# One FFN input chunk in two parts around an attention product, in a fused linear-attention and FFN kernel

## The chip, the core and the metric

The kernel runs on one core of a Trainium2 chip. The metric is the device time of one execution in microseconds. Five engines work side by side, each with an instruction queue of its own: TensorE (PE; its weight loads are shown as PEld), VectorE (DVE), ScalarE (ACT), GpSimd (POOL) and SyncE (SP, which here only issues transfers). All times below are in microseconds.

## The reference

A linear attention over 8 batches of 8 heads, 576 positions and 64 features, and behind it an FFN with an ELU between its two products.

```python
q_s = exp(q - max(q, -1));  q_s = q_s / (sum(q_s, -1) + 1e-9)
k_s = exp(k - max(k, 2));   k_s = k_s / (sum(k_s, 2) + 1e-9)
kv = einsum('bhsd,bhse->bhde', k_s, v)
attn = einsum('bhsd,bhde->bhse', q_s, kv)
x = attn.transpose(0, 2, 1, 3).reshape(4608, 512)
h = x @ w_in                                  # 512 -> 2048
g = where(h > 0, h, exp(min(h, 0)) - 1)
out = g @ w_out                               # 2048 -> 512
```

## The kernel before

**Steps.** The program goes batch by batch, and each batch (j from 0) in 16 steps, one for each chunk of 128 of the 2048 hidden features; 16 more steps at the end handle the positions that each batch leaves over. Chunks are numbered through: n = 16 j + c, so that chunk 16 is the first one of the second batch. Each chunk has four pieces of work:

- *h(n)*, the FFN input product (hidden_mm, L912): four matmuls, kc = 0 to 3, each contracting 128 of the 512 model features and all adding up in one PSUM bank (banks 0 to 2 by turns). Matmul kc reads quarter kc of the batch's attention output, tile XT.
- *E(n)*, the exponential on ACT (L895, for some chunks L892 and L893) and, for the L895 chunks, a subtraction of 1 on POOL (L896), into tile ES.
- *elu(n)* on VectorE (L925), which joins the two into tile GT.
- *p(n)*, the output product (project, L933): four matmuls, t = 0 to 3, which add onto banks 3 to 6, where a batch's output grows over its 16 chunks.

TensorE's order is h(n) and then p(n - 3), step by step: h15, p12, h16, p13, h17, p14 and so on. After p15 the first batch's output is complete, and its four banks are evicted, banks 3 and 5 by ACT (L942), banks 4 and 6 by VectorE (L944), and stored by SP. p16 is the first product that writes these banks again, behind h19.

**The attention of the next batch** runs in the gaps of these steps. Its last part is four products, att:f (attend, L805), one matmul each, which all write bank 7, and four copies, xc:f (xcopy, L814, on ACT), which bring bank 7 to quarter f of XT. Since they share the bank, att:f waits for the xc before it. They come in the order 0, 1, 3, 2.

**The order** on every engine is written out by hand. A table (FIRST for the steps of the first batch, SECOND for the second's) gives for each step three lists of words: the first is done behind h(n) and its E(n), the second behind p(n - 3), the third behind elu(n). An engine's queue is in program order. One semaphore wait stands ahead of each instruction that needs another engine's result.

In the last two steps of FIRST there are also, for the third batch: join2 (kpeak_join, a chain of small VectorE operations that ends in tile KU, L413), kout2 (kpeak_out, L417: a transfer of KU to memory, issued from ACT's queue), and load:V:2:MR (transfers on SP's queue). In the first steps of SECOND VectorE takes the maxima of queries (qmax, L672) and POOL subtracts them (qsub, L679).

Of the kernel before, what the change touches and what calls it, by code (L numbers as in the profile page):

```python
# [14 lines left out]
NCH = DFF // 128  # L15
# [10 lines left out]
LAG = 3  # L26
HELD = ((8, 6), (8, 9), (8, 12))
HB = (0, 1, 2)
EARLY = 4
FINE = 1  # L30
OB = (3, 4, 5, 6)
# [32 lines left out]
    12: ("pturn:B w2:15:16", "pwide:B:act load:Q:2:ABR", "w2:13:15"),  # L64
    13: ("kv:A vconv:B:dve", "kfac:A:dve", "kexp:B peak2:B att:0 xc:0"),
    14: ("kv:B kfac:B:dve peak2:R qmulr:gp", "att:1 peak2:A", "join2 turn:R xc:1"),
    15: ("att:3", "xc:3", "att:2 load:V:2:MR xc:2 kout2"),
}
SECOND = {
    0: ("qmax:C qsub:D", "", "qmax:A"),  # L70
# [50 lines left out]
class Gen:  # L121
# [754 lines left out]
    def hbank(self, n):  # L876

        if n < EARLY:
            return HB[n] if n < len(HB) else AB
        return HB[(n - EARLY) % len(HB)]  # L880

    def hidden(self, j, c):

        a, g = self.E["act"], self.E["gp"]
        n = j * NCH + c
        bank = self.hbank(n)
        ps, ES = self.bank[bank], self.ES[n % NE]
        self.hidden_mm(j, c, range(2, 4) if n < EARLY else range(4))
        for x, keys in self.pieces("ES", n, NE):
            mark = ["FINE"] if n < FINE else []  # L890
            if n in AT["clip"]:
                self.op("act", lambda: a.activation(ES[:, x], ps[:, x], AF.Relu, scale=-1.0), [f"bank{bank}"], keys + mark)  # L892
                self.op("act", lambda: a.activation(ES[:, x], ES[:, x], AF.Exp, scale=-1.0), keys, keys)  # L893
                continue
            self.op("act", lambda: a.activation(ES[:, x], ps[:, x], AF.Exp), [f"bank{bank}"], keys + mark)  # L895
            self.op("gp", lambda: g.tensor_scalar(ES[:, x], ES[:, x], -1.0, 1.0, ALU.add, ALU.mult),  # L896
                    keys, keys)
# [6 lines left out]
    def hidden_mm(self, j, c, kcs):  # L904
        pe = self.E["pe"]
        bank = self.hbank(j * NCH + c)
        x = self.XT[j % 2] if j < B else self.XTR
        xkeys = [self.xkeys(j, (f,), "LH") for f in range(4)] if j < B else [[f"XTR{b}" for b in range(B)]] * 4
        ps = self.bank[bank][:, :]
        for kc in kcs:  # L910
            def mm():
                return pe.matmul(ps, self.W1S[:, kc, c * 128:(c + 1) * 128], x[:, kc, 0:SM],  # L912
                                 start=(kc == 0), stop=(kc == 3))
            self.hidden_done = self.op("pe", mm, xkeys[kc] + [f"W1_{c}"],
                                       [f"bank{bank}"])

# [67 lines left out]
    def finish(self, first):  # L984
# [7 lines left out]
        for t in range(3):  # L992
# [3 lines left out]
            self.store_rest(t, "sp")  # L996
        for i, bank in enumerate((HB[0], AB)):
            for c in last:
# [147 lines left out]
    def program(self):  # L1146
        self.alloc()
        self.init()
        self.first_batch()

        steps = [(j, s) for j in range(B + 1) for s in range(NCH)]
        behind = 0
        for i, (j, s) in enumerate(steps):
            mid, end, after = TABLES.get(j, LATER).get(s, NONE) if j < B else NONE
            self.hidden(j, s)
            self.do(j, mid)
            if i >= LAG and (j, s) not in HELD:
                pj, ps = steps[behind]
                behind += 1
                self.project(pj, ps)  # L1160
                self.do(j, end)
                if ps == NCH - 1:
                    self.store(pj)
            else:
                self.do(j, end)
            self.elu(j, s)
            self.do(j, after)
        self.finish(steps[behind][1])
        for name in self.sems:
            if name.startswith("d_OSB"):  # L1170
                self.E["sp"].wait_ge(self.sems[name], self.count[name])
# [36 lines left out]
```

## Time and profile before

| what | value |
|---|---|
| runs shown | 308.54, 308.96 (median), 309.47 |
| the profiled execution | 309.2, of which the span of the profile is 307.4 |
| granted TensorE clock | 1.0 of full speed |
| TensorE busy | 298.6 |
| VectorE, ACT, POOL busy | 234.8, 193.1, 171.8 |
| where chunk 16 lies in the span | h16 from 53.92, E16 from 55.56, elu 16 from 57.00 |

Two views of the profile carry what follows. The chain of waits is followed back from the last instruction: each piece names what it was that the end waited for. Its rows are start, length, and the engine and line. The timeline's rows are start, length, engine, line, operation, tiles and how many instructions were merged; in brackets stands how long the engine had been idle and what released it. Starts count from the beginning of the span. A matmul's length holds its way through the array; the next one starts before it ends.

### The profile page before, as it was taken

Reading aid. Unit: us, or ns where it says so; the run is one execution under the profiler, and the core shown is the slowest. Engines: PE = TensorE matmul, PEld = TensorE weight load, DVE = VectorE, ACT = ScalarE, POOL = GpSimd, SP = SyncE. Lnnn points to the kernel's source line nnn. Section 1 sums busy time; section 2 is a strip of 40 time slices with the busy share of each in tenths; the row PEclk is TensorE's granted clock in tenths of the full one; section 3 lists DMA queues with packets and bytes.
Section 4 is the critical chain, followed back from the end, with each engine's and each line's share of the span. In section 5 each row is a group of like instructions: output and inputs, shape, how many; then the busy total and the mean of one; then the engine's idle time right before and its main releaser. Section 6 shows DMA issues by size and latency. Waiting matters only on the chain.

```text
span 307.4 us, 4838 instructions
## 1 busy us (share of the span) xinstructions
PE 298.6 (97%) x1733; PEld 240.5 (78%) x1733; DVE 234.8 (76%) x400; ACT 193.1 (63%) x358; POOL 171.8 (56%) x215
## 2 busy tenths in 40 slices
PE   7789999999999999999999999999999999999995
PEld 5467877788878888888888888888888888888884
DVE  6888988979959897999799988998895353335442
ACT  2588885586559684967487758775877543334432
POOL 2877884687437643785378627863786333333440
PEclk9999999999999999999999999999999999999999
DMA  7999999994708993768475846590512030003004
GB/s 233 396 345 373 377 350 265 297 265 115 188 15 250 258 254 102 226 126 230 121 230 135 218 126 221 139 197 0 173 29 51 2 136 0 0 2 136 0 0 136
DMA packets 60071, 51.63 MB, mean 168 GB/s; under 512 B 26896, under 2 KB 50192, under 8 KB 60048
## 3 DMA queue, kind: packets, MB, share of 16 engines
q1 hardware_dynamic: 52960, 41.23, 48.0%
q0 software_dynamic: 5888, 8.39, 10.1%
q10 hardware_dynamic: 1200, 1.72, 2.0%
q8 instruction: 13, 0.21, 0.3%
q14 instruction: 10, 0.08, 0.1%
HBM read 38.27 MB, written 9.45 MB: 155 GB/s over the span
## 4 chain that ended last, share of the span: by engine, by line
PE 91%; POOL 3%; DVE 2%; DMA 2%; issue 1%; SPq 1%; ACT 0%
PE bank L933 43%; PE bank L912 42%; PE bank L827 2%; DMA QR<-in_q_dram 2%; PE bank L598 1%; POOL W1S L255 1%; DVE KT L326 1%; POOL QR L679 1%; PE bank L560 1%; SPq L277 1%; PE bank L805 1%; POOL W2S L262 0%; POOL VB L857 0%; DVE QM L672 0%; PE bank L1007 0%
## 5 line engine op out<-in xcount | busy, mean ns | idle before, releaser
L933 PE MATMUL bank<-W2S,GT 128*128 128x512 f32 x572 | 153.4, 391 | 0.1
L896 POOL TENSOR_SCALAR ES<-ES 128x512 f32<-128x512 f32 (+1 forms) x130 | 86.3, 666 | 115.8 <-ACT ES L895 115.8
L912 PE MATMUL bank<-XT,W1S 128*128 128x512 f32 x512 | 138.5, 393 | 0.5 <-issue 0.2
L925 DVE SCALAR_TENSOR_TENSOR GT<-bank,ES 128x512 fp32r<-128x512 f32 (+1 forms) x130 | 87.9, 680 | 53.2 <-PE bank L912 40.4
L933 PEld LDWEIGHTS bank<-W2S,GT 128*128 128x128 f32 x572 | 106.3, 188 | 22.0 <-DVE GT L925 0.6
L895 ACT ACTIVATE ES<-bank 128x512 f32<-128x512 f32 (+1 forms) x130 | 76.1, 593 | 70.5 <-PE bank L912 70.4
L912 PEld LDWEIGHTS bank<-XT,W1S 128*128 128x128 f32 x512 | 94.0, 188 | 20.0 <-ACT XT L814 0.9
L679 POOL TENSOR_TENSOR QR<-QR,QM 128x512 f32<-128x512 f32 (+1 forms) x21 | 24.9, 1190 | 1.0 <-DVE QM L672 1.0
L684 ACT ACTIVATE QR<-QR 128x1024 f32<-128x1024 f32 (+3 forms) x19 | 19.0, 1007 | 3.5 <-DVE QR L679 3.5
L855 ACT ACTIVATE XT<-bank 128x320 fp32r<-128x320 f32 (+1 forms) x30 | 15.1, 502 | 9.4 <-PE bank L827 9.2
L689 DVE TENSOR_REDUCE QZ<-QR 128x16 f32<-128x1024 f32 (+1 forms) x14 | 18.8, 1343 | 0.6 <-ACT QR L684 0.6
L672 DVE TENSOR_REDUCE QM<-QR 128x16 f32<-128x1024 f32 (+1 forms) x14 | 18.8, 1344 | 0.3 <-DMA QR<-in_q_dram 0.3
L912 PE MATMUL bank<-XTR,W1S 128*128 128x512 f32 x64 | 16.6, 389 | 0.0
L438 DVE TENSOR_TENSOR KR<-KR,NB 128x512 f32<-128x512 f32 x16 | 14.6, 936 | 0.0
L623 ACT ACTIVATE MB<-bank,KZ 64x64 fp32r<-64x64 f32 x44 | 10.1, 302 | 7.0 <-DVE KZ L614 6.9
L387 DVE TRANSPOSE_TENSOR_REDUCE KM<-KR 128x32 f32<-128x1024 f32 x12 | 14.4, 1224 | 0.0
L912 PEld LDWEIGHTS bank<-XTR,W1S 128*128 128x128 f32 x64 | 12.0, 188 | 2.5
L857 POOL CAST QT<-QW 128x1024 fp32r<-128x1024 f16 x12 | 12.5, 1045 | 2.5 <-DMA QW<-QS 2.5
L827 PE MATMUL bank<-QT,MB 128*128 128x320 f32 (+1 forms) x48 | 12.6, 302 | 0.7 <-ACT XT L855 0.7
L892 ACT ACTIVATE ES<-bank 128x512 f32<-128x512 f32 x15 | 8.9, 595 | 6.4 <-PE bank L912 6.4
L708 POOL TENSOR_TENSOR QS<-QR,QI 128x1024 f16<-128x1024 f32 (+1 forms) x7 | 12.5, 1790 | 0.3 <-DVE QI L691 0.3
L484 ACT ACTIVATE EK<-KR 128x1024 bf16<-128x1024 f32 x12 | 12.6, 1050 | 0.0
(108 smaller groups left out, 264.3 us busy)
## 6 DMA issues: line engine op xcount, KB each, us to landing
out_dram<-OSB SPq DMA_DIRECT2D x30, 256.0 KB, 2.8
KR<-in_k_dram SPq DMA_DIRECT2D x6, 1024.0 KB, 8.2
VR<-in_v_dram SPq DMA_DIRECT2D x6, 1024.0 KB, 6.3
QR<-in_q_dram SPq DMA_DIRECT2D x5, 1024.0 KB, 8.0
W2S<-in_moe_w_out_dram POOLq DMA_DIRECT2D x5, 512.0 KB, 11.4
KR<-in_k_dram SPq DMA_DIRECT2D x8, 288.0 KB, 6.4
VR<-in_v_dram SPq DMA_DIRECT2D x8, 288.0 KB, 6.5
W1S<-in_moe_w_in_dram POOLq DMA_DIRECT2D x3, 768.0 KB, 9.5
```

What stands on the lines that cost most here:

```text
L438: self.op(en, lambda: e.tensor_tensor(kv, kv, m, ALU.subtract), keys + ["NB"], keys)
L672: self.op("dve", lambda: v.tensor_reduce(m, QR, AX.X, ALU.max), self.qkeys(b, part), self.qstat("QM", b, part))
L679: self.op(en, lambda: e.tensor_tensor(QR, QR, m, ALU.subtract), keys + self.qstat("QM", b, part), self.qown(b, part))
L684: self.op("act", lambda: a.activation(QR, QR, AF.Exp), keys, self.qown(b, part))
L689: self.op("dve", lambda: v.tensor_reduce(z, QR, AX.X, ALU.add), self.qkeys(b, part), self.qstat("QZ", b, part))
L827: last = pe.matmul(self.bank[bank][:, a - c0:b - c0], self.MB[f][:, :, :].rearrange("p u d -> p (u d)"), self.QT[:, f, a - f * S:b - f * S ...
L855: self.op("act", lambda: e.activation(out, src, AF.Copy), reads, writes)
L895: self.op("act", lambda: a.activation(ES[:, x], ps[:, x], AF.Exp), [f"bank{bank}"], keys + mark)
L896: self.op("gp", lambda: g.tensor_scalar(ES[:, x], ES[:, x], -1.0, 1.0, ALU.add, ALU.mult), keys, keys)
L912: return pe.matmul(ps, self.W1S[:, kc, c * 128:(c + 1) * 128], x[:, kc, 0:SM], start=(kc == 0), stop=(kc == 3))
L925: self.op("dve", lambda: v.scalar_tensor_tensor(out[:, x], *how), [f"bank{bank}"] + eks + (["FINE"] if n < FINE else []), keys)
L933: return pe.matmul(self.bank[OB[t]][:, :], self.GT[n % NG][:, t * 128:(t + 1) * 128], self.W2S[:, c, :], start=(c == 0), stop=(c == NCH - ...
```

## The change

Three things are edited. The words att:2 and xc:2 leave the third list of step 15; load:V and kout2 stay there. In step 16 the product h16 is issued as kc 0, 1 and 3, then att:2 and xc:2 follow, then p13, then kc 2 as the last one of the group, and only then E16. And the flag that closes the group in PSUM moves with it from kc 3 to kc 2. Every matmul, copy and transfer is still there; the order of the sum over kc is 0, 1, 3, 2 for this one chunk.

```diff
+LATE = (NCH, ((0, 1, 3), (2,)), "att:2 xc:2")
...
-    15: ("att:3", "xc:3", "att:2 load:V:2:MR xc:2 kout2"),
+    15: ("att:3", "xc:3", "load:V:2:MR kout2"),
...
     def hidden(self, j, c):
 
+        n = j * NCH + c
+        if n == LATE[0]:
+            first, late = LATE[1]
+            self.hidden_mm(j, c, first)
+            self.do(j - 1, LATE[2])
+            return late
+        self.hidden_mm(j, c, range(2, 4) if n < EARLY else range(4))
+        self.hidden_exp(j, c)
+
+    def hidden_exp(self, j, c):
...
+        end = LATE[1][1][-1] if j * NCH + c == LATE[0] else 3
         for kc in kcs:
             def mm():
                 return pe.matmul(ps, self.W1S[:, kc, c * 128:(c + 1) * 128], x[:, kc, 0:SM],
-                                 start=(kc == 0), stop=(kc == 3))
+                                 start=(kc == 0), stop=(kc == end))
...
-            self.hidden(j, s)
+            late = self.hidden(j, s)
+            if late:
+                self.project(*steps[behind])
+                behind += 1
+                self.hidden_mm(j, s, late)
+                self.hidden_exp(j, s)
+                self.do(j, mid)
+                self.do(j, end)
+                self.elu(j, s)
+                self.do(j, after)
+                continue
```

(hidden_exp is the rest of what hidden was.)

TensorE's queue from the end of p12 (GT0) to h17 (bank 1), before; bank 7 takes att:2, bank 0 takes h16, and banks 3 to 6 with GT1 are p13:

```order
L933 MATMUL bank6<-W2S,GT0 128x512
L805 MATMUL bank7<-QT,MB 128x512
L912 MATMUL bank0<-XT1,W1S 128x512 x4
L933 MATMUL bank3<-W2S,GT1 128x512
L933 MATMUL bank4<-W2S,GT1 128x512
L933 MATMUL bank5<-W2S,GT1 128x512
L933 MATMUL bank6<-W2S,GT1 128x512
L912 MATMUL bank1<-XT1,W1S 128x512 x4
```

The same stretch of the changed kernel, whose lines have moved (L945 is project, L806 attend, L924 hidden_mm):

```order
L945 MATMUL bank6<-W2S,GT0 128x512
L924 MATMUL bank0<-XT1,W1S 128x512 x3
L806 MATMUL bank7<-QT,MB 128x512
L945 MATMUL bank3<-W2S,GT1 128x512
L945 MATMUL bank4<-W2S,GT1 128x512
L945 MATMUL bank5<-W2S,GT1 128x512
L945 MATMUL bank6<-W2S,GT1 128x512
L924 MATMUL bank0<-XT1,W1S 128x512
L924 MATMUL bank1<-XT1,W1S 128x512 x4
```

Three matmuls of h16 have moved ahead of att:2, and the fourth behind p13.

ACT's queue at the same place, before: E15 (ES3), then xc:3 and xc:2 (two copies of bank 7 to XT1), kout2, E16 (ES0) and E17:

```order
L895 ACTIVATE ES3<-bank2 128x512
L814 ACTIVATE XT1<-bank7 128x512 x2
L417 DMA kmax_scratch<-KU 16x32
L895 ACTIVATE ES0<-bank0 128x512
L892 ACTIVATE ES1<-bank1 128x512
```

And of the changed kernel:

```order
L906 ACTIVATE ES3<-bank2 128x512
L815 ACTIVATE XT1<-bank7 128x512
L418 DMA kmax_scratch<-KU 16x32
L815 ACTIVATE XT1<-bank7 128x512
L906 ACTIVATE ES0<-bank0 128x512
L903 ACTIVATE ES1<-bank1 128x512
```

The second copy, xc:2, has moved behind kout2. On VectorE, POOL and SP the order is what it was.

More of the change, by code (lines that the diff above doesn't have):

```diff
@@ L887, in hidden @@
         ps, ES = self.bank[bank], self.ES[n % NE]
-        self.hidden_mm(j, c, range(2, 4) if n < EARLY else range(4))
         for x, keys in self.pieces("ES", n, NE):
```

## The prediction

> **What bounds the kernel now.** I read the page's busy shares and chain first, then the chain of waits in order of time around the first chunk of the second batch, then the timeline of every engine there.
>
> ```profile
> span 307.4 us, 4838 instructions
> PE 298.6 (97%) x1733; PEld 240.5 (78%) x1733; DVE 234.8 (76%) x400; ACT 193.1 (63%) x358; POOL 171.8 (56%) x215
> PE 91%; POOL 3%; DVE 2%; DMA 2%; issue 1%; SPq 1%; ACT 0%
> ```
>
> TensorE is busy nearly always and is 91% of the chain. A TensorE gap that is closed is worth its length, one that is opened costs its length, and other engines matter only where TensorE waits for them. The chain at the changed place:
>
> ```profile
> 52.66 0.93 PE bank L933 x4
> 53.59 0.51 PE bank L805
> 54.10 0.02 issue
> 54.12 0.61 ACT XT L814
> 54.73 0.04 issue
> 54.77 0.73 PE bank L912 x2
> 55.50 0.93 PE bank L933 x4
> ```
>
> After p12 comes att:2 (L805), then the chain leaves TensorE for xc:2 (ACT, L814) and returns with the last two matmuls of h16 (kc 2 and 3). This is the stall that the change can reach. The same stretch on the timeline:
>
> ```profile
> 52.50 1.09 PE L933 MATMUL bank<-W2S,GT 128*128 128x512 f32 x4
> 52.94 0.59 ACT L814 ACTIVATE XT<-bank 128x512 fp32r<-128x512 f32 x1
> 53.58 0.19 PEld L805 LDWEIGHTS bank<-QT,MB 128*128 128x128 f32 x1 [0.43 <-ACT XT L814]
> 53.58 0.50 PE L805 MATMUL bank<-QT,MB 128*128 128x512 f32 x1
> 53.92 0.62 PE L912 MATMUL bank<-XT,W1S 128*128 128x512 f32 x2
> 54.12 0.60 ACT L814 ACTIVATE XT<-bank 128x512 fp32r<-128x512 f32 x1 [0.59 <-PE bank L805]
> 54.77 0.30 PEld L912 LDWEIGHTS bank<-XT,W1S 128*128 128x128 f32 x2 [0.66 <-ACT XT L814]
> 54.91 0.20 DVE L413 STREAM_TRANSPOSE KU<-KQ 32x32 f32<-32x32 f32 x1
> 55.14 0.36 ACTq L417 DMA_DIRECT2D kmax_scratch<-KU  x1
> 55.34 1.09 PE L933 MATMUL bank<-W2S,GT 128*128 128x512 f32 x4
> 55.56 0.60 ACT L895 ACTIVATE ES<-bank 128x512 f32<-128x512 f32 x1 [0.84 <-PE bank L912]
> 56.27 1.07 PE L912 MATMUL bank<-XT,W1S 128*128 128x512 f32 x4
> 57.18 1.07 PE L933 MATMUL bank<-W2S,GT 128*128 128x512 f32 x4
> 60.80 1.07 PE L933 MATMUL bank<-W2S,GT 128*128 128x512 f32 x4
> ```
>
> Undisturbed, four matmuls take 57.18 - 56.27 = 0.91, so 0.227 each. A matmul whose weight load had to wait takes more: att:2 starts at 53.58 and the next at 53.92, 0.34, so 0.11 of its load lies bare; kc 2 and 3 of h16 took 55.34 - 54.77 = 0.57, again 2 x 0.227 and 0.11. From p12 (52.50) to h17 (56.27) there are 13 matmuls; at 0.227 they take 2.95, and they took 3.77. The loss is 0.82: 0.17 at att:2, which waits for xc:3 to free bank 7, 0.11 behind it, 0.51 at kc 2, which waits for xc:2, and the rest in p13.
>
> **What the change removes.** Behind p12 now stand kc 0, 1 and 3 of h16. They start at 52.50 + 0.91 = 53.41, 53.64 and 53.86. kc 3 needs xc:3, done at 52.94 + 0.59 = 53.53, while its weights load 0.23 ahead of it, at 53.63: no wait. att:2 follows at 54.09, with bank 7 free since 53.53: no wait. p13 runs 54.32 to 55.22, and kc 2 could start at 55.22 and h17 at 55.45. That would be the whole 0.82. att:2's result would be there after its 0.39 to 0.50, at about 54.55 by the later; xc:2 could run 54.55 to 55.15. On TensorE's side the cover is enough, just.
>
> **What the change adds: xc:2 stands behind kout2.** On ACT's queue the order was xc:3, xc:2, kout2, E16; it becomes xc:3, kout2, xc:2, E16, since kout2 stayed in the table of step 15 and xc:2 went to the next step. kout2 waits for KU, the last of VectorE's join2 chain, ready at 54.91 + 0.20 = 55.11; it is issued at 55.14, and that takes 0.36. Before, only E16 stood behind it, and E16 waited for h16 until 55.50 anyway. Now the copy on which kc 2 depends stands there. KU does not move: nothing that the change touches is ahead of it on VectorE.
>
> How long the issue itself holds ACT the trace does not show, since no activation was ready behind one. It lies between 0 and 0.36. The nearest rows are POOL's:
>
> ```profile
> 45.28 1.66 POOL L262 DMA_DIRECT2D W2S<-in_moe_w_out_dram  x2
> 46.21 0.60 ACT L895 ACTIVATE ES<-bank 128x512 f32<-128x512 f32 x1 [0.66 <-PE bank L912]
> 46.97 0.63 POOL L896 TENSOR_SCALAR ES<-ES 128x512 f32<-128x512 f32 x1
> ```
>
> POOL's operation had its input at 46.21 + 0.60 = 46.81 and started at 46.97, behind the end of the issues at 46.94. So an issue holds what is queued behind it, and I take 0.36: xc:2 starts at 55.14 + 0.36 + 0.02 = 55.52 and ends at 56.12; kc 2 starts 0.05 later (the step from 54.72 to 54.77 before), at 56.17, and h17 0.34 behind it, at 56.51. Before it was 56.27: **plus 0.24**. With a hold of 0, xc:2 runs 55.16 to 55.76, kc 2 starts at 55.81 and h17 at 56.15: minus 0.12.
>
> [...]
>
> **What is late next: E16 and VectorE.** Chunk 16 is complete only with kc 2, and everything of VectorE's step 16 stands behind its elu.
>
> ```profile
> 56.24 0.62 POOL L896 TENSOR_SCALAR ES<-ES 128x512 f32<-128x512 f32 x1 [2.50 <-ACT ES L895]
> 57.00 0.67 DVE L925 SCALAR_TENSOR_TENSOR GT<-bank,ES 128x512 fp32r<-128x512 f32 x1
> 57.60 1.20 DVE L672 TENSOR_REDUCE QM<-QR 128x16 f32<-128x1024 f32 x1
> 58.73 0.27 DVE L857 CAST QT<-QWR 128x256 fp32r<-128x256 f16 x1
> 58.92 0.67 DVE L925 SCALAR_TENSOR_TENSOR GT<-ES,bank 128x512 fp32r<-128x512 f32 x1
> 59.65 1.29 DVE L944 COPY OSB<-bank 128x512 f32<-128x512 f32 x2
> 60.85 0.68 DVE L925 SCALAR_TENSOR_TENSOR GT<-bank,ES 128x512 fp32r<-128x512 f32 x1
> 62.42 0.69 DVE L925 SCALAR_TENSOR_TENSOR GT<-bank,ES 128x512 fp32r<-128x512 f32 x1 [0.88 <-PE bank L912]
> 65.00 0.69 DVE L925 SCALAR_TENSOR_TENSOR GT<-bank,ES 128x512 fp32r<-128x512 f32 x1 [0.48 <-PE bank L864]
> ```
>
> kc 2 ends 0.50 after its start (as att:2 did), at 56.67; E16 starts 0.06 later (55.50 to 55.56 before), at 56.73; POOL's part, 0.68 after E16's start (55.56 to 56.24), at 57.41, ending at 58.03; elu 16 at 58.07. It was at 57.00: VectorE is 1.07 late. Behind elu 16 it has no gap: a maximum of queries, a cast, elu 17, then the two evictions of the first batch's banks 4 and 6, at 59.65. Of the 1.07 it absorbs 0.13 there: the first eviction stands 0.73 behind elu 17's start (58.92), where an elu needs only 0.60 (57.00 to 57.60). Each eviction takes half of 1.29 and a little overlap, so they end at about 61.27 and 61.88 instead of 60.33 and 60.94.
>
> They matter because p16 writes those banks. p16 starts at 60.80 before, its second and fourth matmuls at 61.03 and 61.48, so the slack was 0.70 and 0.54. With TensorE 0.24 late they come due at 61.27 and 61.72. The second can load its weights at 61.27 + 0.04, with 0.11 bare, and counts from 61.42: 0.15 lost. The fourth is then due at 61.87 and counts from 61.88 + 0.15 = 62.03: another 0.16. Together **plus 0.3**. Its bounds: 0, if VectorE catches up before the evictions, and 0.83, all of the 1.07 beyond the 0.24. With a hold of 0, VectorE is 0.71 late and TensorE 0.12 early, so both sides move by the same 0.36 and the loss stays 0.3.
>
> After that VectorE has 0.88 of idle time before 62.42 and 0.48 before 65.00, more than its remaining lag against TensorE (0.94 - 0.54), so I let nothing more be lost. POOL becomes late too, since the query subtractions stand behind its part of chunk 16:
>
> ```profile
> 57.16 1.48 POOL L679 TENSOR_TENSOR QR<-QR,QM 128x768 f32<-128x768 f32 x1 [0.29 <-DVE QM L672]
> 60.48 1.04 POOL L679 TENSOR_TENSOR QR<-QR,QM 128x512 f32<-128x512 f32 x1
> ```
>
> That makes elu 19 and 20 late by up to the same 1.07; p19 and p20 read them three steps, 3 x 2 x 0.91 = 5.5, behind h19 and h20, so nothing of it reaches TensorE. What else is moved costs nothing: the load of V on SP's queue stands where it stood, and no matmul, activation or transfer is added.
>
> **The sum.** The profiled execution took 309.2 (span 307.4): 309.2 + 0.24 + 0.3 = 309.75. It lies 0.24 above the median of the runs, 308.96, so against the median: 308.96 + 0.54 = **309.5**.
>
> **The rivals.**
>
> 1. *The hold is near 0, or the evictions are not reached.* Minus 0.12 + 0.3 = +0.2, or +0.24 alone: 309.2. For it: no row shows ACT held by an issue; the slack of 0.54 is nearly enough. Against it: POOL's rows.
> 2. *The gain is kept* (the other side): xc:2 does not stand behind kout2's wait, on ACT, and decides if it can start before about 54.6. h17 starts 0.82 early, but the evictions then bind: elu 17 starts at 58.92 whatever TensorE does, so they end at most 0.13 earlier, at 60.20 and 60.81, while p16's second matmul is due at 61.03 - 0.82 = 60.21, counts from 60.20 + 0.15 and loses 0.14, the fourth another 0.16. Net -0.82 + 0.3 = minus 0.5: 308.4. Against it: KU is ready at 55.11, and for a full gain would have to be 0.9 earlier.
> 3. *The lag spreads.* All of VectorE's 1.07 reaches TensorE, by the evictions or by elu 17 to 19 behind POOL's subtractions: +1.07, 310.0. It decides if VectorE cannot use the 0.88 and 0.48 of idle time since POOL is late as well (VectorE's wait before 62.42 was for chunk 19, in whose way POOL's subtractions stand).
>
> **How the numbers follow.** The forecast 0.5, rival 1 0.2, rival 2 0.1, rival 3 0.2. About 0.3%, 0.93 us, is what a measurement of this kernel can tell from no change (its runs lie within 308.54 to 309.47). The forecast (+0.54) and rivals 1 and 2 lie inside it, rival 3 (+1.07) outside. Slower by more takes rival 3's 0.2 and 0.06 of the forecast, whose eviction term can be nearer its upper bound of 0.83; faster by more takes half of rival 2, 0.05; the rest, 0.69, is within. The range runs from 308.6 to 310.2: it leaves out most of rival 2 below and a tenth above, where the lag spreads and more comes to it; it holds a hold of 0 with no loss at the evictions (308.96 - 0.12 = 308.84) and rival 3. The forecast's own is 309.1 to 309.9.
>
> **What would show it.** Right: the issue of kout2 stands on ACT's queue at about 55.14, xc:2 starts at about 55.5 behind it, TensorE waits some 0.9 at kc 2 and h17 starts near 56.5; elu 16 near 58.1; the weight loads of p16 wait for VectorE's evictions (L944 before). Wrong: xc:2 starts at 54.6; or att:2 or kc 3 waits; or p16 runs without a wait; or TensorE waits for an elu (L925 before) between 62 and 70.

## The result, and the profile after

| kernel | median | runs | range |
|---|---|---|---|
| before | 309.19 | 22 | 308.21 to 309.74 |
| changed | 309.88 | 22 | 309.26 to 311.09 |

The ratio is 1.0022, with a 95% interval of 1.0014 to 1.0029: the change costs 0.69 us, between 0.43 and 0.90. The forecast was +0.54, so 309.5, with a range of 308.6 to 310.2, in which the measured 309.88 lies. The profiled execution of the changed kernel took 309.67, of which 307.9 is the span, where it was 309.2 and 307.4.

The page's chain by engine in the changed kernel, which was PE 91% before:

```profile
PE 89%; DVE 3%; POOL 3%; DMA 2%; issue 1%; SPq 1%; ACT 0%; ACTq 0%
```

The chain of waits of the changed kernel, in order of time, at the changed place (start, length, what):

```profile
54.80 0.21 DVE KU L414
55.01 0.02 issue
55.03 0.37 ACTq L418
55.40 0.05 issue
55.45 0.61 ACT XT L815
56.05 0.04 issue
56.10 1.45 PE bank L924 x5
```

Before, it left TensorE here only for one copy of 0.61. Now it runs through VectorE's KU, kout2's issue from ACT's queue (ACTq) and xc:2, and all of that sets the start of kc 2. ACTq is new in the page's chain. The timeline of the same stretch, TensorE, ACT and VectorE, up to h20 (62.25) and elu 19 (63.27):

```profile
52.32 0.60 ACT L906 ACTIVATE ES<-bank 128x512 f32<-128x512 f32 x1 [0.33 <-PE bank L924]
52.38 1.09 PE L945 MATMUL bank<-W2S,GT 128*128 128x512 f32 x4
53.30 0.86 PE L924 MATMUL bank<-XT,W1S 128*128 128x512 f32 x3
54.00 0.40 PE L806 MATMUL bank<-QT,MB 128*128 128x512 f32 x1
54.24 1.09 PE L945 MATMUL bank<-W2S,GT 128*128 128x512 f32 x4
55.45 0.60 ACT L815 ACTIVATE XT<-bank 128x512 fp32r<-128x512 f32 x1 [2.04 <-PE bank L945]
56.10 1.45 PE L924 MATMUL bank<-XT,W1S 128*128 128x512 f32 x5 [0.77 <-ACT XT L815]
58.05 0.69 DVE L937 SCALAR_TENSOR_TENSOR GT<-bank,ES 128x512 fp32r<-128x512 f32 x1 [1.08 <-PE bank L945]
60.58 1.28 DVE L956 COPY OSB<-bank 128x512 f32<-128x512 f32 x2
61.03 1.38 PE L945 MATMUL bank<-W2S,GT 128*128 128x512 f32 x4
61.23 0.60 ACT L906 ACTIVATE ES<-bank 128x512 f32<-128x512 f32 x1 [0.24 <-PE bank L924]
61.31 0.30 PEld L945 LDWEIGHTS bank<-W2S,GT 128*128 128x128 f32 x2 [0.32 <-DVE OSB L956]
61.91 0.19 PEld L945 LDWEIGHTS bank<-W2S,GT 128*128 128x128 f32 x1 [0.30 <-DVE OSB L956]
62.25 1.09 PE L924 MATMUL bank<-XT,W1S 128*128 128x512 f32 x4
63.27 0.69 DVE L937 SCALAR_TENSOR_TENSOR GT<-bank,ES 128x512 fp32r<-128x512 f32 x1 [0.82 <-POOL ES L907]
```

The first stall of the old order is gone: from p12 through three matmuls of h16, att:2 and p13 there is no gap. Then TensorE is idle for 0.77 before kc 2, which by the start of p13 could have begun at 54.24 + 0.91 = 55.15 and is 0.95 late. A second stall has come 5 us later: two weight loads of p16 wait 0.32 and 0.30 for VectorE's evictions (L956), and the four matmuls of p16 take 62.25 - 61.03 = 1.22 instead of 0.91. The wait of 2.04 in the row of xc:2 is put down to p13 (L945), which is not what held it: att:2 had ended at 54.40. It is kout2's place in the queue, which the chain shows.

For the rest, all kernels are compared from the exponential of chunk 15 (E15), the last one ahead of the change, since what lies before it is the same program and yet shifts by some tenths from one execution to the next. E15 starts at 52.44 in the kernel before and 52.32 in the changed one; E19 at 61.01 and 61.23, so 0.34 later against E15; E21 at 64.63 and 65.19, so 0.68 later; the end of the span 0.6 later. What is lost by E21 stays lost, and nothing is added to it. The rows of E15, E19 and E21 before, and of E21 after:

```profile
52.44 0.60 ACT L895 ACTIVATE ES<-bank 128x512 f32<-128x512 f32 x1 [0.33 <-PE bank L912]
61.01 0.60 ACT L895 ACTIVATE ES<-bank 128x512 f32<-128x512 f32 x1 [0.23 <-PE bank L912]
64.63 0.60 ACT L892 ACTIVATE ES<-bank 128x512 f32<-128x512 f32 x1 [1.21 <-PE bank L912]
...
65.19 0.60 ACT L903 ACTIVATE ES<-bank 128x512 f32<-128x512 f32 x1 [1.02 <-PE bank L924]
```

### The profile page after: what moved, and what is told of

Its sections match the earlier page's. It is cut to its first block, busy times and chain, and to the rows that moved or that the text cites. A ratio compares the mean times of both kernels' runs of the same rounds, so it can differ in the third digit from the quotient of the medians.

```text
span 307.9 us, 4838 instructions
## 1 busy us (share of the span) xinstructions
PE 297.7 (97%) x1733; PEld 240.3 (78%) x1733; DVE 234.9 (76%) x400; ACT 193.0 (63%) x358; POOL 171.7 (56%) x215
## 4 chain that ended last, share of the span: by engine, by line
PE 89%; DVE 3%; POOL 3%; DMA 2%; issue 1%; SPq 1%; ACT 0%; ACTq 0%
PE bank L945 42%; PE bank L924 41%; PE bank L828 2%; DMA QR<-in_q_dram 2%; PE bank L599 1%; POOL W1S L256 1%; DVE KT L327 1%; POOL QR L680 1%; PE bank L561 1%; SPq L278 1%; DVE KM L388 0%; POOL W2S L263 0%; POOL VB L858 0%; DVE GT L937 0%; DVE QM L673 0%
## 5 line engine op out<-in xcount | busy, mean ns | idle before, releaser
L945 PE MATMUL bank<-W2S,GT 128*128 128x512 f32 x572 | 153.6, 392 | 0.1
L924 PE MATMUL bank<-XT,W1S 128*128 128x512 f32 x512 | 138.2, 392 | 1.0 <-ACT XT L815 0.8
L937 DVE SCALAR_TENSOR_TENSOR GT<-bank,ES 128x512 fp32r<-128x512 f32 (+1 forms) x130 | 87.8, 681 | 54.2 <-PE bank L924 39.5
L945 PEld LDWEIGHTS bank<-W2S,GT 128*128 128x128 f32 x572 | 106.2, 188 | 22.5 <-DVE OSB L956 0.6
L924 PEld LDWEIGHTS bank<-XT,W1S 128*128 128x128 f32 x512 | 94.1, 188 | 20.4 <-ACT XT L815 1.4
L680 POOL TENSOR_TENSOR QR<-QR,QM 128x512 f32<-128x512 f32 (+1 forms) x21 | 24.9, 1190 | 0.8 <-DVE QM L673 0.8
L673 DVE TENSOR_REDUCE QM<-QR 128x16 f32<-128x1024 f32 (+1 forms) x14 | 18.8, 1341 | 0.1
L924 PE MATMUL bank<-XTR,W1S 128*128 128x512 f32 x64 | 16.6, 389 | 0.0
L858 POOL CAST QT<-QW 128x1024 fp32r<-128x1024 f16 x12 | 12.5, 1042 | 2.9 <-DMA QW<-QS 2.9
L924 PEld LDWEIGHTS bank<-XTR,W1S 128*128 128x128 f32 x64 | 12.0, 188 | 2.5
```

The lines of the kernel that those rows point to most:

```text
L673: self.op("dve", lambda: v.tensor_reduce(m, QR, AX.X, ALU.max), self.qkeys(b, part), self.qstat("QM", b, part))
L680: self.op(en, lambda: e.tensor_tensor(QR, QR, m, ALU.subtract), keys + self.qstat("QM", b, part), self.qown(b, part))
L937: self.op("dve", lambda: v.scalar_tensor_tensor(out[:, x], *how), [f"bank{bank}"] + eks + (["FINE"] if n < FINE else []), keys)
L945: return pe.matmul(self.bank[OB[t]][:, :], self.GT[n % NG][:, t * 128:(t + 1) * 128], self.W2S[:, c, :], start=(c == 0), stop=(c == NCH - ...
```

## The experiments

Each ratio is against the kernel before, run on the same chip in the same job (medians of before: 308.93 for e1 to e4, 309.17 for e5 to e7). The last two columns give how much later than in the kernel before E19 and E21 start, counted from E15, in the one profiled execution; they are taken before rounding, so the rounded rows can differ by 0.01.

| run | median | ratio, 95% interval | E19 | E21 |
|---|---|---|---|---|
| changed | 309.88 | 1.0022, 1.0014 to 1.0029 | +0.34 | +0.68 |
| e1 kout2 behind xc:2 | 308.92 | 1.000, 0.9991 to 1.0009 | -0.71 | -0.33 |
| e2 maximum first | 309.35 | 1.0018, 1.0009 to 1.0027 | +0.28 | +0.28 |
| e3 wait without issue | 309.30 | 1.0015, 1.0006 to 1.0024 | -0.12 | +0.27 |
| e4 kout2 alone | 310.59 | 1.0069, 1.0047 to 1.0092 | +3.05 | +3.05 |
| e5 e1 with one eviction on ACT | 308.54 | 0.998, 0.9969 to 0.9991 | -0.55 | -0.47 |
| e6 that eviction alone | 309.02 | 0.9993, 0.9983 to 1.0003 | +0.11 | +0.01 |
| e7 e1 again | 308.79 | 0.9987, 0.9978 to 0.9996 | -0.75 | -0.37 |

### e1: kout2 behind xc:2

```diff
-LATE = (NCH, ((0, 1, 3), (2,)), "att:2 xc:2")
+LATE = (NCH, ((0, 1, 3), (2,)), "att:2 xc:2 kout2")
...
-    15: ("att:3", "xc:3", "load:V:2:MR kout2"),
+    15: ("att:3", "xc:3", "load:V:2:MR"),
```

> The changed kernel with kout2 put back behind xc:2 on ACT's queue. Theory (xc:2 is held by kout2's wait for KU and by its issue): xc:2 starts at about 54.5, kc 2 waits 0.1 or not at all, h17 starts some 0.75 earlier than in the kernel before; VectorE's evictions then bind p16 for about 0.3; against the kernel before -0.5 us, ratio near 0.9985; against the changed kernel -1.2 us. Rival (the wait at kc 2 comes from the moved product itself, and kout2's place is no matter): as the changed kernel, ratio near 1.002.

The timeline of e1, with E15 at 52.62:

```profile
54.54 1.09 PE L945 MATMUL bank<-W2S,GT 128*128 128x512 f32 x4
54.74 0.60 ACT L815 ACTIVATE XT<-bank 128x512 fp32r<-128x512 f32 x1 [1.03 <-PE bank L806]
55.34 0.36 ACTq L418 DMA_DIRECT2D kmax_scratch<-KU  x1
55.47 1.34 PE L924 MATMUL bank<-XT,W1S 128*128 128x512 f32 x5
59.86 1.28 DVE L956 COPY OSB<-bank 128x512 f32<-128x512 f32 x2
60.28 1.41 PE L945 MATMUL bank<-W2S,GT 128*128 128x512 f32 x4
```

xc:2 starts as soon as att:2 is there (0.03 behind its end, 54.31 + 0.40 = 54.71), and kc 2 follows p13 without a gap (54.54 + 0.91 = 55.45, and it starts at 55.47). E19 is 0.71 early: the two-part product does remove the old stall. But the row of p16 is now 1.41 long against the 1.07 of an undisturbed group of four, since VectorE's evictions bind it: they start 7.24 behind E15, where they started 7.21 behind it before (59.65 - 52.44). Of the 0.71 only 0.33 is left at E21. The timing, 1.000 where 0.9985 was expected, did not show even that, though it does rule out the rival's 1.002; the kernel is timed again in e7.

### e2: the second maximum ahead of elu 16

```diff
-    0: ("qmax:C qsub:D", "", "qmax:A"),
+    0: ("qmax:C qsub:D qmax:A", "", ""),
```

> The changed kernel with the second query maximum of step 16 put ahead of elu 16 on VectorE, where VectorE stood idle for 1.08. Theory (the second half of the loss is VectorE's lag reaching p16 through the evictions): elu 16 near 58.1 as before, elu 17 near 59.0, evictions end near 60.6 and 61.2, p16 does not wait; -0.3 us against the changed kernel, ratio to the kernel before near 1.0012. Rival (p16 waits for something else, or the lag only moves on): ratio stays near 1.002.

The timeline of e2, with E15 at 51.56; L673 are the two maxima, L680 are two subtractions on POOL, L937 is elu 16, L858 the cast, then come the evictions, p16 and h20:

```profile
54.73 2.59 DVE L673 TENSOR_REDUCE QM<-QR 128x20 f32<-128x1280 f32 x2
57.13 2.53 POOL L680 TENSOR_TENSOR QR<-QR,QM 128x768 f32<-128x768 f32 x2
57.27 0.69 DVE L937 SCALAR_TENSOR_TENSOR GT<-bank,ES 128x512 fp32r<-128x512 f32 x1
57.88 0.88 DVE L858 CAST QT<-QWR 128x256 fp32r<-128x256 f16 x1
59.28 1.28 DVE L956 COPY OSB<-bank 128x512 f32<-128x512 f32 x2
60.21 1.07 PE L945 MATMUL bank<-W2S,GT 128*128 128x512 f32 x4
61.12 1.07 PE L924 MATMUL bank<-XT,W1S 128*128 128x512 f32 x4
```

The maximum fills the 1.08 in which VectorE had waited. elu 16 stands where it stood (57.27 - 51.56 = 5.71 behind E15; 5.73 in the changed kernel), but the evictions start 7.72 behind E15 instead of 8.26, and p16 runs in 0.91. E21's lag falls from 0.68 to 0.28, and from E19 to E21 nothing is added, where 0.34 was. So the second half of the loss came by VectorE's evictions. One expectation was missed: elu 17 was to come near 59.0 in the changed kernel's time and came at 59.44, since the cast ahead of it took 0.88 and not 0.28. POOL's two subtractions, between which there was a gap of 0.56 in the changed kernel, now ran beside the cast all that time; no run here shows whether that is the cause. The timing can't decide: 1.0009 to 1.0027 holds the 1.0012 of the theory and the 1.002 of the rival. The reading rests on the profile.

### e3: the wait without the issue

```diff
-LATE = (NCH, ((0, 1, 3), (2,)), "att:2 xc:2")
+LATE = (NCH, ((0, 1, 3), (2,)), "att:2 xc:2 kout2")
...
-    15: ("att:3", "xc:3", "load:V:2:MR kout2"),
+    15: ("att:3", "xc:3", "load:V:2:MR kwait"),
...
+            elif name == "kwait":
+                self.need("act", self.writer["KU"])
```

> The changed kernel with kout2's issue behind xc:2, but with ACT's wait for KU left ahead of xc:2. It parts the wait from the issue. If an issue holds ACT for its whole 0.37: xc:2 starts near 55.06 instead of 55.45, h17 and the end 0.37 earlier than in the changed kernel, ratio to the kernel before near 1.001. If the issue holds nothing and the wait alone does it: xc:2 stays near 55.4 and the ratio near 1.002.

The timeline of e3, with E15 at 52.41: KU, then xc:2, then the issue.

```profile
54.90 0.20 DVE L414 STREAM_TRANSPOSE KU<-KQ 32x32 f32<-32x32 f32 x1
55.13 0.60 ACT L815 ACTIVATE XT<-bank 128x512 fp32r<-128x512 f32 x1 [1.63 <-DVE KU L414]
55.14 0.36 ACTq L418 DMA_DIRECT2D kmax_scratch<-KU  x1
55.78 1.42 PE L924 MATMUL bank<-XT,W1S 128*128 128x512 f32 x5 [0.37 <-ACT XT L815]
```

xc:2 starts 0.03 behind KU's end and 55.13 - 52.41 = 2.72 behind E15; in the changed kernel it is 3.13. The issue of 0.37 thus holds what is queued behind it on ACT for 0.41. E21's lag shrinks by the same 0.41, from 0.68 to 0.27. The issue behind xc:2 costs nothing here: it runs beside the copy, and E16 behind it waits for kc 2 anyway. The timing, 1.0006 to 1.0024, holds both expected ratios, so this too rests on the profile.

### e4: kout2's place alone

```diff
-    15: ("att:3", "xc:3", "att:2 load:V:2:MR xc:2 kout2"),
+    15: ("att:3", "xc:3", "att:2 load:V:2:MR kout2 xc:2"),
```

> The kernel before with one word moved: kout2 ahead of xc:2, h16 whole and where it was. Theory: xc:2 starts near 55.5 instead of 54.12, kc 2 waits 1.4 longer; VectorE is late by about as much as TensorE, so p16 does not wait: +1.4 us, ratio near 1.0045. Rival (ACT lets xc:2 pass): ratio 1.000.

The wait is there as expected, but it brought a second cost with it. The timeline of e4 from kc 2 and 3 of h16 on, and its busy times by stretch (busy and count of each engine, then the granted clock, PEclk):

```profile
56.00 0.94 PE L912 MATMUL bank<-XT,W1S 128*128 128x512 f32 x2 [1.65 <-ACT XT L814]
56.74 1.91 PE L933 MATMUL bank<-W2S,GT 128*128 128x512 f32 x4
58.45 1.71 PE L912 MATMUL bank<-XT,W1S 128*128 128x512 f32 x4
...
54.00:56.00 2.00, 0.35 (x2) 0.00 (x1) 1.87 (x7) 0.60 (x1) 0.00 (x0) 1.00 0.89 251
56.00:58.00 2.00, 2.00 (x5) 1.58 (x6) 0.87 (x1) 0.60 (x1) 0.34 (x1) 0.59 1.14 341
58.00:60.00 2.00, 2.00 (x7) 1.54 (x6) 1.62 (x2) 0.00 (x0) 1.72 (x2) 0.56 1.10 308
60.00:64.00 4.00, 4.00 (x19) 3.30 (x18) 2.59 (x6) 2.96 (x6) 2.32 (x3) 1.00 0.45 127
```

TensorE was idle for 1.65. Behind the end of that, its granted clock fell: the stretches from 56 to 58 and from 58 to 60 have a mean of 0.59 and 0.56, and those on both sides, from 54 to 56 and from 60 to 64, have 1.00. By the two means the clock lacked 2.00 x 0.41 + 2.00 x 0.44 = 1.70 at full speed. p13 took 58.45 - 56.74 = 1.71 where four matmuls take 0.91. E21 is 3.05 late. kc 2 starts 1.43 later against E15 than before, which is the expected wait; the other 1.6 fits the 1.70 that the clock lacked. Not every execution shows it. Two of the six runs list a mean granted clock of 0.992 and took 312.08 and 312.34; the other four list 0.999 or 1.0 and took 310.31 to 310.63, which is 1.4 to 1.7 above the median of before, as expected of the wait alone (the 1.0069 of the table takes in all six). p16 (63.65, with h20 at 64.56) does not wait, as expected. The rival, that ACT lets xc:2 pass, is out.

### e5, e6 and e7: what e1 gave back

e5 is e1 and the eviction of the first batch's bank 6 on ACT; e6 is the kernel before with that eviction alone; e7 is e1's kernel again, measured beside them.

```diff
-            self.evict(t, ("act", "dve")[t % 2])
+            self.evict(t, "dve" if t == 1 or (t == 3 and j) else "act")
```

> The changed kernel with kout2 behind xc:2, as in e1, and with the first batch's eviction of bank 6 moved from VectorE to ACT, which has 0.24 to spare behind its two. Theory (what e1 gained at kc 2, 0.7 in its profile, it gave back to 0.34 at p16 by VectorE's two evictions): one eviction less on VectorE takes the fourth matmul's wait away and leaves 0.1 at the second; chunk 21's exponential stands 0.6 to 0.7 earlier against chunk 15's than in the kernel before; ratio to the kernel before near 0.998, below e1's in the same job by 0.3 us or so. Rival (a gain at this place does not reach the end): ratio 1.000, as e1's first measurement.

> The kernel before with only the eviction of the first batch's bank 6 moved from VectorE to ACT. Control: in the kernel before p16 has 0.5 of slack on that eviction, so by the theory nothing is gained, 0.0 us, ratio 1.000. If this alone makes it faster, the gain of e5 is not that of the product in two parts.

> The kernel of e1 once more. Its first measurement, 1.000 with an interval of 0.9991 to 1.0009, stands against its own profile, in which the stretch from chunk 15 to the end is 0.34 us shorter than in the kernel before. Theory: 0.9988, so the two measurements together lie below 1. Rival (the saving is lost in places that one profile doesn't show): 1.000 again.

The timeline of e5, with E15 at 52.50:

```profile
59.08 1.57 ACT L954 ACTIVATE OSB<-bank 128x512 f32<-128x512 f32 x3
59.75 0.68 DVE L956 COPY OSB<-bank 128x512 f32<-128x512 f32 x1
60.20 1.25 PE L945 MATMUL bank<-W2S,GT 128*128 128x512 f32 x4
61.29 1.08 PE L924 MATMUL bank<-XT,W1S 128*128 128x512 f32 x4
```

p16 takes 61.29 - 60.20 = 1.09 instead of e1's 61.53 - 60.28 = 1.25, so half of what it gave back is kept; the second matmul still waits for the one eviction that VectorE has left, for 0.18 where 0.1 was expected. E21 is 0.47 early, not the 0.6 to 0.7 expected. The ratio, 0.998 with 0.9969 to 0.9991, is as expected and below 1. Against e7, which is e1's kernel in the same job, the median is lower by 0.25, but the two intervals overlap; that this eviction gains on top of e1 rests on the profile. The control e6 is not told apart from 1 (0.9993, 0.9983 to 1.0003), and its E21 stands at +0.01: the eviction alone gives nothing that shows. e7, 0.9987 with 0.9978 to 0.9996, agrees with the -0.33 and -0.37 of the two profiles; e1's first interval, 0.9991 to 1.0009, just leaves out the 0.9989 or less that they amount to. The two profiles put the gain of e1's kernel at a third of a microsecond; the medians of the two timings, 0.01 and 0.38 below those of before, put it at 0.2. It is small, and its size is not settled.

## Why the prediction was right

- **The old stall goes.** Right. No wait at kc 3, att:2 or p13, as worked out. In e1, where nothing else is in the way, E19 is 0.71 to 0.75 early; 0.75 was expected there, after the 0.82 of the prediction.
- **xc:2 is held behind kout2's wait and issue.** Right. xc:2 was forecast 3.08 behind E15 and came 3.13 behind, kc 2 at 3.73 and came at 3.78; TensorE is 0.34 late at E19, where 0.24 was forecast. That ACT would not let xc:2 pass kout2 was the author's assumption, which no row of the kernel before shows; e4, which moves that word alone, shows it: kout2's issue ended at 54.94 + 0.36 = 55.30 and xc:2 started at 55.35, though att:2 had ended at 53.38 + 0.50 = 53.88. Half of the missing tenth is there at kc 2: the issue took 0.37 and not 0.36, and the step from its end to xc:2 was 0.05 and not 0.02. The rest was lost by hundredths in the matmuls from kc 2 to h19.
- **The hold of the issue**, bounded by 0 and 0.36 and taken as 0.36 by a row of POOL's: e3 measured 0.41, just above the upper bound. The choice of the upper end was right, and rival 1 with a hold near 0 is out.
- **The evictions.** Forecast to lose 0.15 and 0.16 at p16's second and fourth matmul; the two waits are there, and p16 takes 0.31 longer. elu 16 was forecast 5.63 behind E15 and came at 5.73. TensorE too was a tenth later than forecast, so the two errors cancel in the wait of p16; that it came out to the hundredth is luck. e2 takes this term away by filling VectorE's idle 1.08.
- **The lag goes no further.** Right in the result: from E21 to the end nothing more is lost, so rival 3 is out. Of the two reasons given, the first did not hold. VectorE did not catch up in the idle time before elu 19 (0.88 before), because POOL was late as well, as rival 3 had it: VectorE waited for POOL nearly as long (0.82, the last row of the timeline after). Counted from E15, elu 19 came 0.97 and elu 20 0.98 later than before, and only elu 21 was back at TensorE's 0.68. The second reason, that p19 and p20 come three steps behind h19 and h20, is what kept this from TensorE: elu 19 ended at 63.96, and p19 started at 67.45.
- **Rival 2** did not happen, but its price was nearly right where e1 made it happen: forecast minus 0.5 after p16's loss, in the profiles -0.33 and -0.37, in the timings -0.01 and -0.38. The gain ahead of p16 was put at 0.82 and was 0.71 to 0.75; the loss from E19 to E21 was put at 0.30 and was 0.38.
- **The sum.** +0.54 forecast, +0.69 measured, 0.43 to 0.90. The forecast time lies 0.4 below the measured median; 0.23 of that is the base, since the three runs shown had a median of 308.96 and the 22 have 309.19. The least difference that can be told, put at 0.93 from the spread of those three, was too coarse: with 22 runs of each kernel 0.69 is told apart from nothing.

Left open: the tenths by which the stretch ahead of E15 shifts between executions, which blur every timing here, were not traced to a cause.

## What to carry to other kernels

A copy that is moved to a later word of a queue written out by hand lands behind everything that stayed in the earlier one; list what now stands ahead of it, and for each what it waits for. A transfer's issue that waits for another engine belongs behind the copies that TensorE needs, where in e1 and e3 the issue cost TensorE nothing, while ahead of xc:2 it held the copy for 0.41. And a stall that is taken away is worth only as much as the next engine in line has slack: here a saving of 0.7 met evictions that could not come earlier and shrank to half; with one of them moved as well, 0.47 was left.

## What the runs showed of the hardware

A transfer's issue on ACT's queue (0.37) held the activation behind it for 0.41, wait for KU not counted; the same issue behind the activation delayed nothing that TensorE waited for.

A gap in TensorE of 1.65 was followed, in the profiled execution of e4, by a mean granted clock of 0.59 and 0.56 in two stretches of 2.00, with 1.00 on both sides. That cost about 1.6 more, an estimate from the 3.05 of E21 less the 1.43 of the wait. The means of the whole execution are 0.992 in this and one other run, and 0.999 or 1.0 in the other four of the six. The gap of 0.77 in the changed kernel had no such effect: its clock is 1.00 in each stretch from 54 to 60, and its 22 runs list 0.998 to 1.0. Why the clock fell, and why in two runs of six only, no run here shows.
